# A unit of 192 tokens as the decays' frame, two visits of TensorE a unit, and one named order for a whole program of linear attention and gated MLP

## The chip, the cores and the metric

The kernel runs on one core of a Trainium2 chip. A core has a matrix engine (TensorE, "PE" in the profile; its weight loads run beside the products and are listed as "PEld"), a vector engine (VectorE, "DVE"), a scalar engine (ScalarE, "ACT"), GpSimd ("POOL") and SyncE ("SP"), which here issues the DMA transfers. Each engine works through its own instructions in order; semaphores make one wait for another. Products land in PSUM, which the kernel divides into named banks; all else lives in SBUF.

The metric is the device time of one execution in microseconds. Three runs of the kernel before gave 649.77, 648.35 and 648.44; the median is 648.44.

## The reference

Linear attention with a decay of its own for every feature, and behind it a gated MLP. There are 4 batches, 8 heads, 768 tokens and 48 features a head; the decays alpha lie between 0.8 and 1.0.

```python
for t in range(S):
    state = alpha[:, :, t, :, None] * state + np.einsum('bhd,bhe->bhde', k[:, :, t], v[:, :, t])
    y[:, :, t] = np.einsum('bhd,bhde->bhe', q[:, :, t], state)
x = y.transpose(0, 2, 1, 3).reshape(B * S, H * D)         # 3072 x 384
g = x @ w_gate                                            # 384 x 1536
out = (g * (1.0 / (1.0 + np.exp(-g))) * (x @ w_val)) @ w_out
```

The weights arrive as float64, all else as float32.

## The kernel before, in words

**Attention.** The tokens of a batch are cut into units of 192 tokens (`T`), four a batch and 16 in all; a unit has three chunks of 64 (`C`, `NU`). The eight heads go as four pairs (`G`): in every tile the features of the even head lie on partitions 0 to 47 and those of the odd head on 64 to 111. Inside a frame of tokens the recurrence has a closed form: the key of a token is multiplied by the decays from it to the frame's end, the query of a token is divided by its own decays to the frame's end, and what is left are masked products of 64 by 64 scores; the state before the frame is decayed over the whole frame first. Here the frame is the chunk. For every unit, alpha, k and q are loaded and turned so that tokens run along the columns (L300 on VectorE, L313 on TensorE for the first block); alpha is clamped to 1 ± `ALPHA_DEV` (L347); the first factor of each chunk is taken out (L355, tile `af`), a backward scan gives the keys' factors (L369, tile `Gs`), a reciprocal of each chunk's whole factor feeds the forward scan (L384, in `AT`), keys and queries are multiplied by their factors (L381 on GpSimd or L708 on VectorE; L404), and `Pt` holds the decay over each chunk.

**A chunk** then goes through these steps. The decayed keys are turned to rows, 64 tokens by 48 features (`k_rows` L426 on VectorE: 8 transposes a chunk; the early units on TensorE, L410, with copies on ScalarE). `scores` (L437, L438) makes four pairs of products, even and odd heads side by side, into the bank `sps_bank`; `causal` (L444, VectorE, 2 instructions) masks them into the tile `X` that also holds the decayed queries. `carry` (L470, L471) makes the state after the chunk: the operand `K` holds the keys' rows and an identity, `V` holds the values and the state before, so one product adds both. It goes to the second half of the bank `yps`, and `decay` (L459, VectorE, 2 instructions) multiplies it by `Pt` into the `V` of the next chunk. `outputs` (L479, L480) makes the chunk's outputs from `X` and `V` into the first half of `yps`; ScalarE rounds them (`rows_hi` L487) and VectorE takes what is left over (`rows_lo` L491). When a unit's three chunks are done, ten small DMAs (`repack`, L538; units 0 and 1 go over TensorE instead) put its outputs, heads together, into `xT`, the MLP's input.

**The MLP** works on blocks of 384 tokens, two units each; there are eight. A block has 12 tiles of 128 hidden features, so there are 96 hidden steps. Every float32 operand is split into a high and a low part in float32r, and a product is the sum of three (high by high, high by low, low by high). A hidden step is a gate product `g` and a value product `v` of 9 matmuls of 128 x 384 each (L555), silu on ScalarE (L563), the product with `v` on VectorE (`hidden` L567), the high part on ScalarE (L571), the low part `hl` (L577) on GpSimd in 82 steps and on VectorE in 14, and an out product of 9 matmuls (L596) into three banks. The first two blocks take turns, 7 and 5 tiles at a time, so that weights are wanted at half the pace; what their first 7 tiles gave goes to DRAM and back. The weights come as float64 and are cut to two float32r parts by VectorE (L93, L96, L99), ScalarE (L239) and GpSimd or VectorE (L243), while the first steps run.

**The order.** The work of the first 24 steps, of units 0 to 6 and of all weights stands in a string `ORDER`: each word names an engine (t TensorE, v VectorE, s ScalarE, g GpSimd, y SyncE) and a piece of work, and each engine gets its words in that order. A number and a star are products of 128 x 256 that nobody reads (L667), 131 in all, where TensorE would have little to do. From step 24 on the rest is written as closures, six slots a unit (`stages`, `preps`), spread over nine of a block's twelve steps, and a scheduler of the language's own framework orders the instructions among them. These lines spread it:

```python
for u in range(WU + 1, nun + 1):
    for i in range(2 * NU):
        slots.append(stages(u - 1)[i] + (preps(u)[i] if u < nun else []))
```

All loads and stores go through SyncE's queue.

## Time and profile before

| What | Before |
|---|---|
| median of three runs | 648.44 us |
| profiled execution: span from first to last instruction | 646.5 us |
| TensorE (PE) busy | 607.9 us, 94% |
| VectorE (DVE) busy | 442.3 us, 68% |
| ScalarE (ACT) busy | 238.5 us, 37% |
| GpSimd (POOL) busy | 244.4 us, 38% |
| first gate product of the MLP | 54.1 us into the span |
| gate products' group (L555) | 864 matmuls, 339 ns each by the profile |

The profile is that of one execution, whose span is the time from its first to its last instruction; the median of the runs stands 1.9 us above it. The page gives the busy time of each engine, its share of the span and how many instructions it holds. Matmuls are pipelined, and the end that the profile gives one is modelled: what one of them costs the stream is read from the distance between two starts, not from its length. Groups of instructions read `line engine operation out<-in, shape, count | busy us, mean ns of one | idle time just before them <- what ended most of it`. In the timeline a row is the start in us, the length, engine, line, operation, tiles, shape and, where several follow one another without a break, their count.

### The profile page before, as it was taken

Reading aid. Unit: us, or ns where it says so; the run is one execution under the profiler, and the core shown is the slowest. Engines: PE = TensorE matmul, PEld = TensorE weight load, DVE = VectorE, ACT = ScalarE, POOL = GpSimd, SP = SyncE. Lnnn points to the kernel's source line nnn. Section 1 sums busy time; section 2 is a strip of 40 time slices with the busy share of each in tenths; the row PEclk is TensorE's granted clock in tenths of the full one; section 3 lists DMA queues with packets and bytes.
Section 4 is the critical chain, followed back from the end, with each engine's and each line's share of the span. In section 5 each row is a group of like instructions: output and inputs, shape, how many; then the busy total and the mean of one; then the engine's idle time right before and its main releaser. Section 6 shows DMA issues by size and latency. Waiting matters only on the chain.

```text
span 646.5 us, 13108 instructions
## 1 busy us (share of the span) xinstructions
PE 607.9 (94%) x5097; PEld 553.3 (86%) x5097; DVE 442.3 (68%) x863; ACT 238.5 (37%) x511; POOL 244.4 (38%) x234
## 2 busy tenths in 40 slices
PE   8988797997998999899999999899999999999995
PEld 5768676897897898898989999798989999999995
DVE  6889999999896886965597648865597745311111
ACT  5757576774333132324223331324213221212211
POOL 6225394213111434563355536353355532112120
PEclk9989779999999999999999999899999999999999
DMA  9989953422137432432142512433142211011001
GB/s 210 201 234 258 296 145 74 114 63 69 39 98 194 113 99 49 113 89 65 51 114 59 130 50 63 97 83 71 50 113 64 56 50 39 1 37 38 1 1 42
DMA packets 89286, 60.32 MB, mean 93 GB/s; under 512 B 41600, under 2 KB 87680, under 8 KB 89216
## 3 DMA queue, kind: packets, MB, share of 16 engines
q1 hardware_dynamic: 89216, 59.41, 37.8%
q8 instruction: 42, 0.69, 0.5%
q14 instruction: 28, 0.23, 0.1%
HBM read 45.22 MB, written 5.90 MB: 79 GB/s over the span
## 4 chain that ended last, share of the span: by engine, by line
PE 56%; DVE 14%; SPq 3%; DMA 2%; issue 2%; ACT 1%; POOL 0%; DVEq 0%; ACTq 0%
PE ops L596 18%; PE v L555 16%; PE g L555 16%; DVE K L426 3%; PE sps_bank L437 2%; SPq L538 2%; PE yps L479 2%; PE yps L470 2%; DVE Gs L369 1%; DMA L<-in_alpha_dram 1%; DVE h L567 1%; DVE AT L300 1%; DVE trk L300 1%; DVE V L459 1%; DVE X L444 1%
## 5 line engine op out<-in xcount | busy, mean ns | idle before, releaser
L555 PE MATMUL v<-xT,w 128*128 128x384 f32 x864 | 171.8, 342 | 7.1 <-DVE h L567 7.1
L555 PE MATMUL g<-xT,w 128*128 128x384 f32 x864 | 169.8, 339 | 2.6 <-ACT h L563 2.6
L596 PE MATMUL ops<-w,hh 128*128 128x384 f32 x576 | 167.0, 347 | 0.7 <-POOL w L243 0.7
L555 PEld LDWEIGHTS v<-xT,w 128*128 128x128 f32 x864 | 151.0, 190 | 10.6 <-DVE h L567 7.1
L577 POOL TENSOR_TENSOR hl<-h,hh 128x384 fp32r<-128x384 f32 x82 | 87.1, 1062 | 190.4 <-ACT hh L571 188.4
L555 PEld LDWEIGHTS g<-xT,w 128*128 128x128 f32 x864 | 151.0, 188 | 4.3 <-ACT h L563 3.0
L567 DVE TENSOR_TENSOR h<-h,v 128x384 f32<-128x384 f32 x96 | 52.8, 550 | 135.9 <-PE v L555 132.3
L596 PEld LDWEIGHTS ops<-w,hh 128*128 128x128 f32 x576 | 105.6, 189 | 4.6 <-POOL w L243 1.5
L571 ACT CAST hh<-h 128x384 fp32r<-128x384 f32 x96 | 49.2, 512 | 158.8 <-DVE h L567 153.0
L404 POOL TENSOR_TENSOR X<-trq,AT 48x256 f32<-48x256 f32 x75 | 60.4, 807 | 117.0 <-PE yps L480 78.2
L596 PE MATMUL ops<-w,hl 128*128 128x384 f32 x288 | 98.5, 342 | 2.8 <-DVE hl L577 2.1
L563 ACT ACTIVATE h<-g 128x384 f32<-128x384 f32 x96 | 47.1, 490 | 99.0 <-PE g L555 91.2
L426 DVE STREAM_TRANSPOSE K<-Gs 32x128 f32<-32x128 f32 x240 | 72.7, 303 | 10.7 <-PE yps L471 5.4
L596 PEld LDWEIGHTS ops<-w,hl 128*128 128x128 f32 x288 | 54.5, 189 | 4.9 <-DVE hl L577 3.0
L487 ACT CAST Y<-yps 112x256 fp32r<-112x256 f32 x48 | 17.8, 371 | 76.5 <-DVE V L459 49.4
L444 DVE TENSOR_TENSOR X<-sps_bank,mask 64x256 f32<-64x256 f32 x96 | 40.5, 422 | 4.9 <-PE sps_bank L438 2.3
L437 PEld LDWEIGHTS sps_bank<-X,Gs 48*64 48x64 f32 x384 | 28.3, 139 | 14.2 <-issue 10.0
L437 PE MATMUL sps_bank<-X,Gs 48*64 48x64 f32 x384 | 37.6, 232 | 1.9 <-DVE X L444 1.9
L381 POOL TENSOR_TENSOR Gs<-trk,Gs 128x768 f32<-128x768 f32 x9 | 29.9, 3317 | 19.7 <-DVE Pt L374 19.7
L438 PE MATMUL sps_bank<-X,Gs 48*64 48x64 f32 x384 | 36.3, 231 | 0.2 <-POOL X L404 0.2
L243 POOL TENSOR_TENSOR w<-t,w 128x768 fp32r<-128x768 f32 (+1 forms) x14 | 27.0, 1930 | 21.5 <-ACT w L239 18.0
L479 PE MATMUL yps<-X,V 128*48 128x64 f32 x384 | 31.5, 225 | 3.0 <-DVE X L444 2.2
(109 smaller groups left out, 758.7 us busy)
## 6 DMA issues: line engine op xcount, KB each, us to landing
xT<-Y SPq DMA_DIRECT2D x84, 72.0 KB, 2.2
raw<-in_moe_w_gate_dram SPq DMA_DIRECT2D x12, 384.0 KB, 5.6
raw<-in_moe_w_val_dram SPq DMA_DIRECT2D x12, 384.0 KB, 5.6
raw<-in_moe_w_out_dram SPq DMA_DIRECT2D x12, 384.0 KB, 5.8
V<-in_v_dram SPq DMA_DIRECT2D x96, 48.0 KB, 2.5
L<-in_alpha_dram SPq DMA_DIRECT2D x28, 144.0 KB, 3.3
L<-in_k_dram SPq DMA_DIRECT2D x28, 144.0 KB, 3.0
L<-in_q_dram SPq DMA_DIRECT2D x28, 144.0 KB, 2.8
```

The source lines that it names most:

```text
L404: eng.tensor_tensor(out=X[r, :, j, :], in0=QT[r, :, cs], in1=Fs[r, :, cs], op=ALU.mult)
L426: nc.vector.transpose(out=Ks[(1 - j) * BO + y : (1 - j) * BO + y + 32, :, j, x : x + 32], in_=Kg[j * BO + x : j * BO + x + 32, :, c * C + ...
L437: nc.tensor.matmul(sps[BO : BO + C, g, :], KTt[0:D, cs], X[0:D, g, 0, :], start=True, stop=True)
L438: nc.tensor.matmul(sps[0:C, g, :], KTt[BO : BO + D, cs], X[BO : BO + D, g, 1, :], start=True, stop=True)
L444: nc.vector.tensor_tensor(out=X[r, :, j, :], in0=sps[r], in1=mask[r].unsqueeze(1).to_broadcast([C, G, C]), op=ALU.mult)
L479: nc.tensor.matmul(yps[0:D, g, 0:C], Vd[:, g, 0, :], X[:, g, 0, :], start=True, stop=True)
L555: nc.tensor.matmul(pt, wsp[kind, f][a][:, kt * P : (kt + 1) * P], xT[blk][:, b_, kt, :], start=(n == 0), stop=(n == 3 * KT - 1),)
L563: nc.scalar.activation(h, acc.pop(("g", blk, f)), AF.Silu)
L567: nc.vector.tensor_tensor(out=h, in0=h, in1=acc.pop(("v", blk, f)), op=ALU.mult)
L571: nc.scalar.copy(out=hh, in_=acc["h", blk, f])
L577: eng.tensor_tensor(out=hl, in0=acc.pop(("h", blk, f)), in1=hh.bitcast(F32), op=ALU.subtract)
L596: nc.tensor.matmul(ops[blk][i], h[b_][:, i * P : (i + 1) * P], wsp["o", f][a], start=(first and n == 0), stop=(last and n == 2),)
```

## The change

The frame of the decays becomes the unit of 192 tokens. The scans start and end at unit bounds (`inj` is filled at every 192nd column, no longer at every 64th), so `af` and `Pt` have one column a pair instead of three, and `ALPHA_DEV` goes from 0.25 to 0.21. Inside a unit a chunk's state needs no decay: it is the state before plus the chunk's keys by values.

- `scores(u)` makes the three chunks' products in one piece (12 pairs, L467 and L468), into two banks (`A0`, half of `A1`).
- `carry(u)` follows (L482, L485): the three chunks' keys by values into parts of `A1` and `A2`, without the state; `K` holds only keys' rows and has one buffer, and `V` holds the values of a whole unit with the state in rows that the product leaves out.
- `causal` is four instructions a unit, two over two chunks (L495, 64 x 512) and two over one (L500, 64 x 256).
- `advance(u, c)` (L514, 2 instructions a chunk) adds the state before the chunk to the carry, into the next chunk's rows of `V`, and for the last chunk into a tile `SE`; in a batch's first unit the first one is a copy (L512), done by ScalarE in all four batches. `decay(u)` (L520), once a unit, multiplies `SE` by `Pt` into the next unit's `V`, on VectorE or GpSimd as the order says.
- `outputs(u)` (L535, L536) makes the three chunks' outputs in one piece, into `A0` and `A1` again, so it waits for the masks and additions of its unit; `rows_hi` and `rows_lo` are two instructions each a unit (L553, L557), written over `X` from unit 2 on.
- `k_rows` turns a unit's keys in 8 transposes of 32 x 384 (L444) from unit 5 on; units 0 to 4 are turned on TensorE. The query products are two a unit (L418).
- The values of a unit are loaded in 6 DMAs at once (L364), when the order says so.

`ORDER` names everything, all 16 units and 96 steps; `stages`, `preps`, the slots and the scheduler's part are gone. Each word names the engine of its work, the low parts of the hidden layer among them (`hl`, 49 on VectorE and 47 on GpSimd), and of the stores of output rows. There are 194 products of 128 x 256 that nobody reads instead of 131, and four of 128 x 512 ahead of the first work.

The hidden layer's products, their splitting and the number of steps stay as they are. This is the core of the diff, with "..." where lines are left out:

```diff
-ALPHA_DEV = 0.25
+ALPHA_DEV = 0.21
...
-    NL, NX, NV, NK, NOT, NY, NTS, WSINGLE = 2, 3, 4, 2, 3, 2, 2, 3
+    NL, NX, NV, NK, NOT, NTS, WSINGLE = 2, 2, 2, 1, 2, 2, 3
...
-    Xt = [cp.tile([P, G, 2, C], F32, name=f"X{i}") for i in range(NX)]
+    Xt = [cp.tile([P, 2, G, T], F32, name=f"X{i}") for i in range(NX)]
...
-        nc.vector.memset(inj[:, C - 1 : W : C], 1.0)
+        nc.vector.memset(inj[:, T - 1 : W : T], 1.0)
...
+    def k_rows(u, i):
+        Ks = k_tile(u)
+        Kg = state[u]["Gs"].rearrange("r (g c t) -> r c g t", g=G, c=NU)
+        j, x = i // 2, 32 * (i % 2)
+        for y in range(0, C, 32):
+            nc.vector.transpose(
+                out=Ks[(1 - j) * BO + y : (1 - j) * BO + y + 32, :, :, x : x + 32],
+                in_=Kg[j * BO + x : j * BO + x + 32, :, :, y : y + 32],
+            )
...
-    def scores(u, c):
+    def scores(u):
...
+        s01 = ps.tile([P, G, 2, C], F32, tag="A0", name=f"s01_{u}")
+        st["A1"] = ps.tile([P, 512], F32, tag="A1", name=f"A1_{u}")
...
+        for c in range(NU):
+            sps = st["sps"][c]
             for g in range(G):
...
+    def carry(u):
...
+        A2 = ps.tile([P, 512], F32, tag="A2", name=f"A2_{u}")
...
+        for c in range(NU - last_of_batch(u)):
+            cps = st["cps"][c]
+            for g in range(G):
+                nc.tensor.matmul(
+                    cps[0:D, g, :], Ks[BO : BO + C, c, g, 0:D], Vd[BO : BO + C, c, g, VC[0]], start=True, stop=True
+                )
+                nc.tensor.matmul(
+                    cps[BO : BO + D, g, :], Ks[0:C, c, g, 0:D], Vd[0:C, c, g, VC[1]], start=True, stop=True
+                )
...
-        if not last_of_batch(u, c):
-            for g in range(G):
-                nc.tensor.matmul(sts[0:D, g, :], Ks[:, g, 0, 0:D], Vd[:, g, 0, :], start=True, stop=True)
...
+    def advance(u, c, eng):
...
+            to = Vd[r, c + 1, :, VC[j]] if c + 1 < NU else SE[r]
...
+                eng.tensor_tensor(out=to, in0=cps[r], in1=Vd[r, c, :, VC[j]], op=ALU.add)
...
+    def outputs(u):
...
+        y01 = ps.tile([P, G, 2, C], F32, tag="A0", name=f"y01_{u}")
+        y2 = ps.tile([P, G, 1, C], F32, tag="A1", name=f"y2_{u}")
...
-    def stages(u):
...
-    for s in range(WS, nsteps + 2):
...
```

What this makes of the engines' instructions is shown at three places. First TensorE, before, around hidden step 25: a gate product (9 matmuls of `g`), pieces of one chunk's scores (`sps_bank`), and the value product between them.

```order
L555 MATMUL g_1_4210<-xT_3628,w_637 128x384 x9
L437 MATMUL sps_bank<-X_96,Gs_3771 64x64
L438 MATMUL sps_bank<-X_96,Gs_3771 64x64
L555 MATMUL v_1_4222<-xT_3628,w_788 128x384 x9
L437 MATMUL sps_bank<-X_96,Gs_3771 64x64
L438 MATMUL sps_bank<-X_96,Gs_3771 64x64
```

After the change TensorE reads thus where unit 12's carries end, at hidden step 64 (the names `A_12` are the three banks, `V` and `K` the unit's values and key rows); 24 instructions of scores and 24 of carries stand ahead of these rows without a product of the MLP among them.

```order
L482 MATMUL A_12_5081<-V_99,K_109 48x48
L485 MATMUL A_12_5081<-V_99,K_109 48x48
L608 MATMUL g_4_5108<-xT_4549,w_1204 128x384 x9
L608 MATMUL v_4_5124<-xT_4549,w_1204 128x384 x9
L608 MATMUL g_5_5137<-xT_4549,w_1311 128x384 x9
L608 MATMUL v_5_5154<-xT_4549,w_1341 128x384 x9
```

A chunk's scores stood in pieces among the products of the MLP; a unit's scores and carries now stand in one piece, and the unit's outputs some products later.

VectorE before, near hidden step 30: turned keys in two buffers (`K_114`, `K_113`), the decay of a chunk's state (`V`), the masks of another chunk (`X`), a whole load turned (`trq`), a low part of outputs (`Y`) and the MLP's hidden product (`h`).

```order
L426 STREAM_TRANSPOSE K_114<-Gs_4195 32x4x32 x8
L426 STREAM_TRANSPOSE K_114<-Gs_4562 32x4x32
L459 TENSOR_TENSOR V_103<-yps,Pt_4199 48x4x48 x2
L426 STREAM_TRANSPOSE K_114<-Gs_4562 32x4x32 x4
L444 TENSOR_TENSOR X_96<-sps_bank,mask 64x4x64 x2
L426 STREAM_TRANSPOSE K_114<-Gs_4562 32x4x32 x3
L300 STREAM_TRANSPOSE trq_4652<-L_71 128x4x6x32
L491 TENSOR_TENSOR Y_4555<-yps,Y_4555 112x4x64
L567 TENSOR_TENSOR h_6_4612<-h_6_4612,v_6_4614 128x384
```

VectorE after, at hidden step 52: the masks of unit 10 over two chunks and over one, keys of unit 11 turned at the width of three chunks (`K_109`), two hidden products, and the additions of the state to the carries (`V<-A_10,V`, and `SE`).

```order
L495 TENSOR_TENSOR X_95<-s_10_4320,mask 64x4x128 x2
L444 STREAM_TRANSPOSE K_109<-Gs_4045 32x12x32 x2
L500 TENSOR_TENSOR X_95<-A_10_4321,mask 64x4x64
L620 TENSOR_TENSOR h_4_4295<-h_4_4295,v_4_4380 128x384
L500 TENSOR_TENSOR X_95<-A_10_4321,mask 64x4x64
L444 STREAM_TRANSPOSE K_109<-Gs_4045 32x12x32 x2
L514 TENSOR_TENSOR V_99<-A_10_4321,V_99 48x4x48 x2
L444 STREAM_TRANSPOSE K_109<-Gs_4045 32x12x32 x2
L620 TENSOR_TENSOR h_5_4377<-h_5_4377,v_5_4408 128x384
L514 TENSOR_TENSOR V_99<-A_10_4351,V_99 48x4x48 x2
```

The masks are wider and fewer, the decay in each chunk has become an addition, key rows come in wider transposes, and all that the unit's outputs wait for stands among keys and hidden products in one queue.

More of the change, by code (lines that the diff above doesn't have):

```diff
@@ L431, in scores @@
[L431 to L443 removed]
+        kps, Ks = state[u].pop(("kps", c)), k_tile(u)
@@ L489, in rows_lo, with rows_of @@
-    def rows_lo(u, c):
-        hi, lo = (state[u]["Y"][:, i, :, c * C : (c + 1) * C] for i in range(2))
-        nc.vector.tensor_tensor(out=lo, in0=yps[0:112, :, 0:C], in1=hi.bitcast(F32), op=ALU.subtract)
-    def stage1(u, c):
-        k_rows(u, c)
-        scores(u, c)
-        causal(u, c)
-    def stage2(u, c):
-        carry(u, c, yps[:, :, C:])
-        outputs(u, c)
-        decay(u, c, yps[:, :, C:])
-        rows_hi(u, c)
-        rows_lo(u, c)
+    def rows_of(u, i, x):
+        cs = slice(0, 2 * C) if i == 0 else slice(2 * C, T)
+        return state[u]["Y"][0:112, x, :, cs].bitcast(F32R), state[u]["yps"][i][0:112].rearrange("r g c t -> r g (c t)")
@@ L734, in named_unit @@
+            todo[f"ad{u}.{c}"] = lambda eng, c=c: advance(u, c, eng)
+        for i in range(4):
+            todo[f"kr{u}.{i}"] = lambda eng, i=i: k_rows(u, i)
+            todo[f"ma{u}.{i}"] = lambda eng, i=i: causal(u, i)
+        todo[f"de{u}"] = lambda eng: decay(u, eng)
+        todo[f"S{u}"] = lambda eng: scores(u)
+        todo[f"B{u}"] = lambda eng: carry(u)
+        todo[f"Y{u}"] = lambda eng: outputs(u)
         for kt in range(KT):
-            todo[f"R{u}{kt}"] = lambda eng, kt=kt: pe_repack(u, kt)
@@ L772, in main_path @@
         named_weights(p)
-    for s in range(WS):
+    for s in range(len(steps)):
         named_step(s)
```

490 lines of the change are left out of this document (231 added, 259 removed).

## The prediction

> **What bounds the kernel now.** I read the page's totals first, then the busy time by stage, then single visits of TensorE to the attention in the timeline, then VectorE's groups.
>
> ```profile
> PE 607.9 (94%) x5097; PEld 553.3 (86%) x5097; DVE 442.3 (68%) x863; ACT 238.5 (37%) x511; POOL 244.4 (38%) x234
> ```
>
> TensorE has no slack over the whole span of 646.5 us. The stages differ, so I cut the span where hidden step 0 and step 17 begin their value products and where the last one does. Columns are the stretch, its length, busy time of each engine, granted clock, DMA.
>
> ```profile
> 0.00:55.80 55.80, 48.13 (x515) 35.78 (x516) 45.13 (x90) 33.80 (x81) 19.59 (x47) 0.97 0.97 218
> 55.80:171.50 115.70, 100.15 (x814) 89.95 (x814) 111.53 (x156) 72.55 (x147) 47.66 (x32) 0.94 0.52 131
> 171.50:634.60 463.10, 454.75 (x3746) 423.13 (x3745) 283.94 (x616) 130.22 (x279) 177.18 (x156) 1.00 0.28 70
> 634.60:646.50 11.90, 4.88 (x28) 4.45 (x26) 1.67 (x3) 1.96 (x4) 0.00 (x0) 0.92 0.17 57
> ```
>
> In the second stretch VectorE is busy 111.5 of 115.7 us (96%): it cuts float64 weights while it prepares units, and it sets the pace. In the third TensorE is busy 454.8 of 463.1 us and VectorE 61%: there TensorE sets the pace. So VectorE work counts from 56 to 171 us, TensorE work from 171 us on.
>
> What a hidden step costs on TensorE alone stands near the end, where no attention is left; these are the first gate products of steps 87 and 88:
>
> ```profile
> 595.58 0.33 PE L555 MATMUL g<-xT,w 128*128 128x384 f32 x1
> ...
> 600.26 0.33 PE L555 MATMUL g<-xT,w 128*128 128x384 f32 x1
> ```
>
> 27 products in 4.68 us, 0.1733 us each. The change leaves all 96 steps as they are. The gate products of steps 24 and 84 bound a long stretch that holds some 30 chunks:
>
> ```profile
> 220.09 0.51 PE L555 MATMUL g<-xT,w 128*128 128x384 f32 x2
> ...
> 581.42 0.33 PE L555 MATMUL g<-xT,w 128*128 128x384 f32 x1
> ```
>
> 361.3 us less 60 steps of 4.68 us leaves 80.5 us, or 8.05 us per 192 tokens of attention. A visit for the scores of one chunk, and one for its carry and outputs, read thus:
>
> ```profile
> 556.05 1.72 PE L555 MATMUL v<-xT,w 128*128 128x384 f32 x9
> 557.70 0.27 PE L437 MATMUL sps_bank<-X,Gs 48*64 48x64 f32 x1
> 557.81 0.22 PE L437 MATMUL sps_bank<-X,Gs 48*64 48x64 f32 x1
> ...
> 558.16 0.22 PE L437 MATMUL sps_bank<-X,Gs 48*64 48x64 f32 x1
> 558.31 0.45 PE L596 MATMUL ops<-w,hh 128*128 128x384 f32 x1
> 558.60 0.34 PE L596 MATMUL ops<-w,hl 128*128 128x384 f32 x1
> ```
>
> ```profile
> 552.45 0.34 PE L596 MATMUL ops<-w,hl 128*128 128x384 f32 x1
> 552.80 0.21 PE L470 MATMUL yps<-V,K 128*48 128x48 f32 x1
> ...
> 553.07 0.21 PE L470 MATMUL yps<-V,K 128*48 128x48 f32 x1
> 553.12 0.22 PE L479 MATMUL yps<-X,V 128*48 128x64 f32 x1
> ...
> 553.51 0.22 PE L479 MATMUL yps<-X,V 128*48 128x64 f32 x1
> 553.67 0.61 PE L596 MATMUL ops<-w,hh 128*128 128x384 f32 x2
> ```
>
> Nine products from 556.05 end their turn at 557.61. The next product starts at 558.31 and its follower 0.29 later, not 0.17: the visit cost 0.70 + 0.11 = 0.81 us. Eight pairs (each float32 product is two instructions, even and odd heads side by side) make the stream, six steps from 557.81 to 558.16, 0.058 us a pair, 0.46 in all. So **0.35 us is the price of entering and leaving**, whatever the visit holds. In the second visit carry pairs step by 0.045 us (six steps from 552.80 to 553.07) and output pairs by 0.056 (seven from 553.12 to 553.51); 552.62 to 553.67 is 1.05 us, 1.15 with the slow follower. A unit done in six clean visits is 3 × (0.81 + 1.15) = 5.9 us. The 2.15 us that the measured 8.05 holds beyond that are visits cut in two by products and waits, such as this one of a carry for the outputs of the chunk before in its bank (waiting line, releaser, total, times, longest):
>
> ```profile
> PE yps L470 <- DVE Y L491: 4.0, 5, 1.4
> ```
>
> **The change, part by part.** First TensorE after step 17. A unit now has one visit of scores and carries, 0.35 + 24 × 0.058 + 24 × 0.045 = 2.8 us, and one of outputs, 0.35 + 24 × 0.056 = 1.7: 4.5 us, against 8.05. The instruction counts per unit stay; what goes is four entries, the cuts, and the wait of a carry for the state, since the carry no longer holds the state and VectorE adds it later. If going from scores to carries cost a whole entry more, a unit would be 4.85. By the named order, outputs of unit 4 and units 5 to 15 come after value product 17: 1.7 + 11 × 4.5 less three carries left out at ends of batches (8 × 0.045 each) = 50 us. With value product 17, 78 further gate and value pairs and 80 out products, 237 × 9 × 0.1733 = 369.7 us of hidden layer are left, so 420 us. Before, the same end was reached thus:
>
> ```profile
> 171.46 0.33 PE L555 MATMUL v<-xT,w 128*128 128x384 f32 x1
> ...
> 639.14 0.34 PE L596 MATMUL ops<-w,hh 128*128 128x384 f32 x1
> ```
>
> That is 467.9 us, with four more out products pending (6.2 us) and 92 us of attention for 34 chunks.
>
> Then VectorE. These groups carry its count (count, busy us, mean ns):
>
> ```profile
> L426 DVE STREAM_TRANSPOSE K<-Gs 32x128 f32<-32x128 f32 x240 | 72.7, 303 | 10.7 <-PE yps L471 5.4 <-PE yps L470 1.1
> L567 DVE TENSOR_TENSOR h<-h,v 128x384 f32<-128x384 f32 x96 | 52.8, 550 | 135.9 <-PE v L555 132.3 <-ACT h L563 2.6 <-issue 0.8
> L444 DVE TENSOR_TENSOR X<-sps_bank,mask 64x256 f32<-64x256 f32 x96 | 40.5, 422 | 4.9 <-PE sps_bank L438 2.3 <-PE sps_bank L667 0.7
> L369 DVE TENSOR_TENSOR_SCAN Gs<-AT,inj 128x768 f32<-128x768 f32 x16 | 31.2, 1953 | 0.7 <-PE kps L410 0.2
> L459 DVE TENSOR_TENSOR V<-yps,Pt 48x192 f32<-48x192 f32 x76 | 27.0, 355 | 3.6 <-PE yps L480 2.4 <-PE yps L471 0.2
> L300 DVE STREAM_TRANSPOSE trk<-L 128x768 f32<-128x768 f32 x14 | 22.4, 1604 | 0.0
> L96 DVE SCALAR_TENSOR_TENSOR t<-raw,t 128x768 uint32<-128x768 uint32 x16 | 19.6, 1223 | 0.3
> L93 DVE TENSOR_SCALAR t<-raw 128x768 uint32<-128x768 uint32 x16 | 11.3, 706 | 0.1
> L577 DVE TENSOR_TENSOR hl<-h,hh 128x384 fp32r<-128x384 f32 x14 | 9.2, 658 | 1.3 <-ACT hh L571 1.2
> L708 DVE TENSOR_TENSOR Gs<-trk,Gs 128x768 f32<-128x768 f32 x2 | 1.9, 942 | 0.0
> ```
>
> Widths 192, 256, 384 and 768 at 355, 422, 550 and 942 ns lie on one line: 0.155 us and 1.04 ns an element. So the causal products of a unit, six of 256 before, are two of 512 (0.69) and two of 256: 2.2 us, 0.3 less. The low parts of the outputs save 0.15, the decays become additions of the same width and save nothing. Key rows turn in 8 transposes of 384 instead of 24 of 128. The rows at 128 and 768 put one at 0.82 us, 6.6 for a unit against 7.3; if nothing were saved it is 0.91. I take 0.82. Low parts of the hidden layer move from GpSimd to VectorE, 49 instead of 14 by the order: 35 × 0.55 (the width's price; the row's 0.66 would make it 23) = 19 us more. So VectorE does not get less to do over the whole; what matters is where.
>
> Between hidden products 0 and 17, counted in both orders: 8 causal products for 22 (4 × 0.69 + 4 × 0.42 against 22 × 0.42) −4.9; 12 additions for 16 decays −1.4; 8 whole transposes for 9 −1.6; 3 low parts of weights for 5 (0.95 by width) −1.9; 3 wide query products for 8 narrow ones (0.94, 0.42) −0.6; 4 low parts of outputs for 8 −1.1; one key product (0.94) and one clamp (0.65, an estimate between the 0.71 row and 0.55) less −1.6; one low part of the hidden layer less −0.6; two passes of the weight cut more, +1.9. Together −11.8 us; part of it only moved behind step 17. TensorE needs 92 us there (50 products of 1.56 us, 11 for attention, a few for fillers and turned keys), so VectorE stays the pace: 115.7 − 11.8, about 104 us. Bounds: 97 (TensorE and some waits) and 110 (half the saving lost in waits).
>
> From hidden product 17 to 40 VectorE has in the new order 32 key transposes (26), 14 whole ones (22), 23 hidden products and 17 low parts (22), 8 scans (15), 18 additions and 4 decays (8), 6 query products (6), 12 causal products (7), 8 low parts of outputs (4) and smaller things (8): 118 us. TensorE needs 123: 69 products of 1.56, the outputs of unit 4 and three units. The slack is nearly gone there. GpSimd gives up the low parts and keeps clamps, decays and weights, off the path. For waits from step 17 on I add 12 us: of the 92 us above 25 are beyond 34 clean chunks of 1.96, and I take half of it for waits (ends 4 and 24).
>
> Start to first value product: VectorE's list up to hidden product 0 differs by under 1 us between the orders. It was busy 45.1 of 55.8 us; 10.7 us were chains and loads. Fillers now stand ahead of the first turned loads, and a unit's chain has one round trip to VectorE instead of three. I take 56 us; half of the idle time gained or lost gives 51 and 61. SyncE's weight loads now stand behind loads that wait for a free buffer, which I cost at nothing: this stretch moved 218 GB/s, and the order cuts the last weights past step 13; a late one would fall within these ends.
>
> The end after the last product start, 7.2 us, stays. **Sum:** 56 + 104 + 420 + 12 + 7.2 = 599 us of span. The median of the runs, 648.44, is 1.9 us over the span of the profiled execution, so 601 us.
>
> **Rivals.** (1) VectorE remains the bound to step 40: nothing saved in the second stretch (116) and 8 us more than TensorE needs in the next. 56 + 116 + 428 + 12 + 7 + 2 = 621 us. For: 118 against 123 us; GpSimd's share stays high. Against: its busy share was 61% there.
>
> (2) The visits are not cheaper because the cost lies in the stream, not the entry: 8.05 us stays per unit, 601 + 11 × 3.55 = 640 us. The 0.35 us read off above speaks against it.
>
> (3) In the carries the two heads of a pair now use different rows of the array (keys at 64 to 127 and at 0 to 63) and write one bank; if they took turns, each pair would be 0.045 longer: 38 chunks × 8 × 0.045 = 14 us, 615 us. The scores of before have the same shape, two row halves and one bank, and step by 0.058 us like the outputs, which use all rows. The Trainium skill, TensorEngine Tiling (Array Packing), section Gotcha 1: PSUM Pressure, says that different row tiles cannot access the same bank at once. By that rule this rival holds; the scores in this trace do not follow it.
>
> (4) Slower: TensorE, in order, stands at each unit's outputs until VectorE has masked the scores and added two states: 2.2 + 4 × 0.355 = 3.6 us after the scores. The cover is the carries (1.05) and the products put between: two (3.1 us) at units 9 and 15, three at 3, 5, 7, 11 and 13, at least four elsewhere. The narrowest has 0.5 us to spare, so VectorE's queue running late is seen at once. It decides from (648 − 601) / 14 = 3.4 us a unit; at 4 us, 657 us. For: hidden products and key transposes stand in the same queue. Against: VectorE idles 39% of that stretch now.
>
> **How the numbers follow.** Forecast 0.70 (582 to 618 with the ends above), rival 1 0.15, rival 2 0.04, rival 3 0.03, rival 4 0.06, and 0.02 that it falls under the range. 0.3% is about what a measurement of this kernel tells from no change. Rivals 1 and 3 are still faster, and rival 2 too; between rival 2 and 4 lies a small 0.02. So faster 0.92, same 0.02, slower 0.06. The range 580 to 624 leaves out the ends of rival 1, and rivals 2 and 4.
>
> **What would show it.** In the new profile two visits a unit of 2.8 and 1.7 us between products; step 17's value product near 159 us, the last product start near 591; carry pairs 0.045 us apart; wide key transposes at 0.82 us. Outputs waiting for causal products or additions by more than 1 us a unit would make it wrong upward, a first value product past 62 us also; VectorE idle between 56 and 159 us would say that its count was not the pace.

## The result, and the profile after

The changed kernel takes 624.5 us, the median of four runs (621.91 to 628.15), against 648.58 for the kernel before. The ratio of the runs is given as 0.9646, with a 95% interval from 0.9603 to 0.9689 (it is not the plain quotient of the two medians, 0.9629): 3.5% faster. The prediction was 601 us (580 to 624): the sign was right, the gain half of what was forecast, and the time lies just above the range. The profiled execution of 624.59 us has a span of 621.9.

First the page's totals of the changed kernel, then its busy time by the prediction's stages (first value product, value product 17, last product).

```profile
PE 580.6 (93%) x5152; PEld 552.6 (89%) x5152; DVE 444.6 (71%) x696; ACT 233.3 (38%) x492; POOL 179.2 (29%) x147
```

```profile
0.00:63.70 63.70, 54.34 (x663) 44.57 (x663) 44.75 (x79) 30.79 (x74) 26.38 (x39) 0.89 0.93 217
63.70:180.90 117.20, 100.33 (x775) 93.26 (x773) 113.02 (x141) 75.14 (x155) 51.96 (x33) 0.96 0.45 120
180.90:615.00 434.10, 425.53 (x3719) 414.64 (x3718) 286.34 (x477) 126.92 (x263) 100.89 (x76) 1.00 0.29 73
```

| Stage | Before | Predicted | After | After less predicted |
|---|---|---|---|---|
| start to first value product | 55.8 | 56 | 63.7 | +7.7 |
| to value product 17 | 115.7 | 104 | 117.2 | +13.2 |
| to the last product | 467.6 | 432 | 434.1 | +2.1 |
| to the end | 7.4 | 7.2 | 6.9 | -0.3 |

The third stage gave 33.5 of the 35.6 us that were forecast. The first two gave back 9.4 us, where 11.5 had been expected to be won: of the 22.7 us by which the span was missed, 20.9 lie ahead of value product 17.

How the third stage is made shows in single visits. These rows of TensorE's timeline in the changed kernel hold both visits to one unit (scores and carries, then outputs), with the products around them.

```profile
464.78 0.69 PE L608 MATMUL v<-xT,w 128*128 128x384 f32 x3
465.40 0.27 PE L467 MATMUL s<-X,Gs 48*64 48x64 f32 x1
...
466.80 0.22 PE L468 MATMUL A<-X,Gs 48*64 48x64 f32 x1
466.85 0.20 PE L485 MATMUL A<-V,K 64*48 64x48 f32 x1
466.85 0.20 PE L482 MATMUL A<-V,K 64*48 64x48 f32 x1
...
467.89 0.20 PE L482 MATMUL A<-V,K 64*48 64x48 f32 x1
468.02 0.45 PE L608 MATMUL g<-xT,w 128*128 128x384 f32 x1
...
471.78 1.21 PE L608 MATMUL g<-xT,w 128*128 128x384 f32 x6
472.91 0.27 PE L535 MATMUL y<-X,V 128*64 128x64 f32 x1
...
474.45 0.44 PE L640 MATMUL ops<-w,hh 128*128 128x384 f32 x1
```

Three products from 464.78 end their turn at 465.30; the next product starts at 468.02, 2.72 us later, 2.83 with its slow follower. Six from 471.78 end at 472.82, the next starts at 474.45: 1.63 us, 1.74 with the follower. Forecast were 2.8 and 1.7. From scores to carries (466.80 to 466.85) nothing is paid. All twelve visits for outputs behind step 17 cost this 1.64 us to 0.01, so none waited. What TensorE did wait for from there to the last product (engine, line, releaser; total, times, longest):

```profile
PE v L608 <- DVE h L620: 5.0, 5, 2.6
PE g L608 <- ACT h L616: 3.5, 3, 1.8
```

### The profile page after: what moved, and what is told of

Read it like the earlier page. It is cut to its first block, busy times and chain, and to the rows that moved or that the text cites. A ratio compares the mean times of both kernels' runs of the same rounds, so it can differ in the third digit from the quotient of the medians.

```text
span 621.9 us, 12936 instructions
## 1 busy us (share of the span) xinstructions
PE 580.6 (93%) x5152; PEld 552.6 (89%) x5152; DVE 444.6 (71%) x696; ACT 233.3 (38%) x492; POOL 179.2 (29%) x147
## 4 chain that ended last, share of the span: by engine, by line
PE 56%; DVE 21%; DMA 9%; SPq 6%; issue 4%; ACT 2%; POOL 1%; DVEq 0%; ACTq 0%; POOLq 0%
PE v L608 16%; PE ops L640 15%; PE g L608 14%; DMA L<-in_alpha_dram 4%; DMA L<-in_k_dram 3%; DVE t L142 2%; SPq L592 2%; DVE K L444 2%; DMA V<-in_v_dram 2%; DVE t L145 2%; DVE h L620 2%; PE s L467 2%; PE y L535 1%; DVE t L139 1%; PE early_ps L681 1%
## 5 line engine op out<-in xcount | busy, mean ns | idle before, releaser
L629 POOL TENSOR_TENSOR hl<-h,hh 128x384 fp32r<-128x384 f32 x47 | 52.8, 1122 | 223.2 <-ACT hh L624 207.6
L620 DVE TENSOR_TENSOR h<-h,v 128x384 f32<-128x384 f32 x96 | 52.9, 551 | 88.0 <-PE v L608 82.4
L418 POOL TENSOR_TENSOR X<-trq,AT 48x768 f32<-48x768 f32 x20 | 40.6, 2030 | 79.5 <-DVE trq L335 25.7
L444 DVE STREAM_TRANSPOSE K<-Gs 32x384 f32<-32x384 f32 x88 | 50.1, 570 | 2.1 <-PE A L485 0.5
L629 DVE TENSOR_TENSOR hl<-h,hh 128x384 fp32r<-128x384 f32 x49 | 33.1, 676 | 18.2 <-ACT hh L624 18.0
L374 ACT ACTIVATE dev<-L,nbias 128x576 bf16<-128x576 f32 (+2 forms) x30 | 23.1, 771 | 39.8 <-DMA L<-in_alpha_dram 30.9
L406 DVE TENSOR_TENSOR_SCAN AT<-AT,inj 128x768 f32<-128x768 f32 x16 | 30.9, 1932 | 0.0
L723 POOL TENSOR_TENSOR Gs<-trk,Gs 128x768 f32<-128x768 f32 x8 | 21.8, 2723 | 31.7 <-DVE Pt L401 31.6
L396 DVE TENSOR_TENSOR_SCAN Gs<-AT,inj 128x768 f32<-128x768 f32 x16 | 28.6, 1786 | 0.6
L495 DVE TENSOR_TENSOR X<-s,mask 64x512 f32<-64x512 f32 x32 | 21.9, 685 | 9.6 <-PE s L468 9.2
L335 DVE STREAM_TRANSPOSE trk<-L 128x768 f32<-128x768 f32 x14 | 22.4, 1600 | 8.7 <-DMA L<-in_k_dram 8.6
```

What stands on the lines that cost most here:

```text
L374: nc.scalar.activation(dev, state[u]["La"][r, cs], AF.Abs, bias=nbias[r], scale=1.0)
L396: nc.vector.tensor_tensor_scan(Gs[:, ::-1], AT[:, 1 : W + 1][:, ::-1], inj[:, 0:W][:, ::-1], 0.0, op0=ALU.mult, op1=ALU.add)
L406: nc.vector.tensor_tensor_scan(AT[:, 0:W], AT[:, 0:W], inj[:, T - 1 : T - 1 + W], 0.0, op0=ALU.mult, op1=ALU.add)
L418: eng.tensor_tensor(out=X[r, j, :, :].rearrange("r g t -> r (g t)"), in0=st["QT"][r, :], in1=AT[r, 0:W], op=ALU.mult)
L444: nc.vector.transpose(out=Ks[(1 - j) * BO + y : (1 - j) * BO + y + 32, :, :, x : x + 32], in_=Kg[j * BO + x : j * BO + x + 32, :, :, y : y ...
L620: nc.vector.tensor_tensor(out=h, in0=h, in1=acc.pop(("v", blk, f)), op=ALU.mult)
```

## The experiments

Each kernel is the changed one with the edit shown; times go with the kernel before on the same chip. Three places are asked about: the price of a visit, the start, and the stretch between hidden products 0 and 17.

### The visits cut again

```diff
-t:S12 t:B12 ... t:g64 ... t:v64 ... t:Y12 ... t:g67
+t:S12a ... t:g64 t:S12b ... t:v64 t:B12 ... t:Y12a ... t:g67 t:Y12b
```

In this kernel the carries come behind the turning of the next unit's keys into the single key buffer, so some of them read those rows: part of the sum is another one.

> The changed kernel with the visits of units 5 to 15 cut again: scores of two chunks, an MLP product, scores of the third, a product, the carries; and outputs of two chunks, a product, outputs of the third. Three more visits a unit, the same matmuls. Theory of the prediction, a visit costs 0.35 us whatever it holds: a unit goes from 4.57 to about 5.6 us, 11 units 11.5 us more, time 634 to 637. Rival, the cost lies in the stream alone: 4.57 us a unit, time 623 to 626. If splitting also brings waits of the outputs, more than 637.

643.43 us, ratio 0.9925 (0.9892 to 0.9958): 19 us more than the change. One unit's carries in its timeline (they stand between these two rows):

```profile
487.77 0.68 PE L613 MATMUL v<-xT,w 128*128 128x384 f32 x3
...
489.60 1.84 PE L613 MATMUL g<-xT,w 128*128 128x384 f32 x9
```

The carries' own visit costs 1.31 + 0.11 us (488.29 to 489.60 and the follower), 1.42 in all. The other four read in the same way cost 1.17 (scores of two chunks), 0.71 (of one), 1.17 (outputs of two) and 0.70 (of one), and 0.11 each: a unit of clean visits is 5.6 us, as the theory of the entry price has it, against 4.57. That is 11 of the 19 us. Most of the rest are waits, and not of the carries, which in all eleven units started 0.27 us behind the start of the product ahead of them: value products waited 9.6 us for hidden products instead of 5.0, and gate products 5.9 us for ScalarE instead of 3.5. Cutting costs the entries and, on top, the slack.

### The start

VectorE's longest waits up to the first value product, in the changed kernel:

```profile
DVE V L514 <- ACT V L512: 4.3, 1, 4.3
DVE AT L380 <- PE pt L348: 4.2, 1, 4.2
DVE trk L335 <- DMA L<-in_k_dram: 2.4, 1, 2.4
```

Three suspects: unit 2's loads (ScalarE checks its alpha ahead of the copies of the first state, VectorE turns its keys), TensorE's fillers, and ScalarE's order.

A first try moved unit 2's keys too early in SyncE's order, over unit 1's queries in the same buffer, before these were turned. So in these two kernels unit 2's keys stand in for unit 1's queries, and TensorE's turn of these waits for a later load, which none of the theories meant. They tell nothing of the loads.

```diff
-t:Tk1 y:wl0 v:cl1 y:wl1 ... y:La2 ... t:Tq1 ... y:Lk2
+t:Tk1 y:La2 y:wl0 v:cl1 y:Lk2 y:wl1 ... t:Tq1
```

> The changed kernel with one edit in SyncE's order: the loads of unit 2's alpha and keys go out ahead of the first weights instead of behind three and four of them. In the changed kernel hidden product 0 stands at 69.6 us, the span is 621.9 us. Loads theory: these two loads, which land at about 28 and 35.5 us, hold ScalarE (its check of alpha, ahead of the copies of the first state) and VectorE (4.3 us for those copies, 2.4 us for the keys); without them VectorE loses 6.7 us less, hidden product 0 comes at about 63, the time falls by 5 to 7 us to about 618. Filler theory: TensorE issues 32 and 26 filler products ahead of unit 0's outputs and unit 1's turned keys, so the outputs still start at 29.5; hidden product 0 comes at 68 to 70 and the time stays at 622 to 625.

> Both edits: the loads of unit 2 ahead of the weights, and fewer filler products. If both hold the start, hidden product 0 comes at 58 to 60 us, where the kernel before has it (58.5), and the time is 612 to 614. If only the loads do, as in the loads edit alone (63 and 618); if only the fillers do, as in the filler edit alone. If VectorE's list of work sets the pace to hidden product 17, whatever is won at hidden product 0 is still there at hidden product 17 (182.7 in the changed kernel).

627.8 us (0.9661) and 623.04 us (0.96). The fillers alone:

```diff
-t:4+ t:10* t:Ta0 ... t:11* ... t:18* ... t:32* t:Y0 ... t:26* ... t:33* t:Y1
+t:10* t:Ta0 ... t:3* ... t:6* ... t:10* t:Y0 ... t:10* ... t:12* t:Y1
```

> The changed kernel with fewer filler products ahead of the first gate product: the four of 512 columns gone, 11, 18, 32, 26 and 33 of 256 columns cut to 3, 6, 10, 10 and 12. Filler theory: TensorE, in order, holds the chain; the first turned load starts at about 4.3 us instead of 7.2, hidden product 0 at 62 to 65 instead of 69.6, the time is about 618. Loads theory: VectorE stands at the loads of unit 2 as before, only longer; hidden product 0 within 1.5 us of 69.6 and the time 623 to 626.

622.41 us, 0.9578 (0.9548 to 0.9608). Hidden product 0 came at 66.1 us, but hidden product 17 at 182.5, where the change has it (182.7): VectorE then stood 3.4 us for unit 3's keys. The loads again, now in an order that keeps the buffers:

```diff
-t:Tk1 y:wl0 ... y:La2 ... t:Tq1 ... y:Lk2 ... y:V3 ... y:Lk3
+t:Tk1 y:La2 y:wl0 ... t:Tq1 y:Lk2 ... y:Lk3 y:V3
```

> The changed kernel with three edits in SyncE's order: unit 2's alpha ahead of the first weights, unit 2's keys right behind the turn of the queries whose buffer they take, unit 3's keys ahead of unit 3's values (six transfers). All is computed as in the changed kernel. Loads theory: VectorE's stands for unit 2 (4.3 us for ScalarE's copies behind its check of alpha, 2.4 us for the keys) go, and unit 3's keys are there in time; hidden product 0 at 63 to 65 instead of 69.6, hidden product 17 about 5 us ahead of 182.7, time 617 to 619. Filler theory: outputs of unit 0 still start behind 32 fillers at 29.5; hidden product 0 at 67 to 70, time 622 to 625. Third possibility: the weights, which go out later, are the next wait, then VectorE or TensorE stands at them and hidden product 17 stays within 2 us of 182.7.

> The same three loads moved, and the fillers cut as in the filler run, which alone brought hidden product 0 from 69.6 to 66.1 and lost it again in a wait of 3.4 us for unit 3's keys. If loads and fillers hold the start and VectorE's list sets the pace to hidden product 17: hidden product 0 at 59 to 62, hidden product 17 at 173 to 177, time 613 to 617. If TensorE and the weights hold the stretch behind hidden product 0: it stays at 179 to 182 and the time at 620 to 622.

620.92 us (0.9551) with the loads alone, hidden product 0 at 67.9, 17 at 182.2: the third possibility, the weights are the next wait. 619.98 us (0.9561, 0.9514 to 0.9608) with both, 64.8 and 178.7, between the two cases expected. The 4.3 us wait was still there with the loads moved: ScalarE now stood 6.4 us for the first weight, which its range check wants. So ScalarE's checks were moved, alone and with the others, the first three weights were put ahead of the values, and the change was run again beside them:

```diff
-s:kc0.1 s:w0c ... s:kc0.2 s:cq1 ... s:ck2.0 ... s:ad0.0 ... s:ck2.1 ... s:yh0.1 y:Lq2
+s:kc0.1 ... s:kc0.2 s:cq1 ... s:ad0.0 ... s:yh0.1 s:w0c s:ck2.0 s:ck2.1 y:Lq2
```

> The changed kernel once more, unaltered, beside the three others. Time 622 to 627 as before; hidden product 0 between 65.9 and 70.3 us, where the profiles with this same start had it. If it lies outside, single profiles of the start tell less than taken.

> The changed kernel with one edit in ScalarE's order: its range checks of the first weight and of unit 2's alpha stand behind unit 0's rounded outputs instead of ahead of the last key copies and of the copies of the first state. Theory that ScalarE's queue holds the start (it stood 2.9 us for the first weight, which goes out at 17.2 us instead of 4.9, and 4.5 us more ahead of the check of alpha): VectorE's stand of 4.3 us for those copies falls under 1 us, TensorE's of 2.0 us for the key copies goes; hidden product 0 comes 2 to 5 us earlier than in the unaltered kernel of this call, the time falls by 1 to 4 us. Filler theory: unit 0's outputs start behind 32 fillers anyway; hidden product 0 within 1.5 us.

> All three edits of the start: ScalarE's checks later, the loads of units 2 and 3 earlier, fewer fillers. Without the checks' move hidden product 0 was at 64.8 and the span 616.4. If ScalarE's checks held what was left: hidden product 0 at 59 to 62, hidden product 17 at 174 to 177, time 614 to 618. If VectorE's list from hidden product 0 to 17 (114 us) is what counts, each us won at hidden product 0 is still there at the end. If the start is then held by transfers: hidden product 0 at 64 to 66 and 619 to 621.

> The same with the first three loads of weights ahead of unit 0's values on SyncE's queue, near 6 us instead of 17 to 21 (the kernel before sends its first at 4.9). If late weights hold the first gate product: it comes 2 us or more ahead of the run with the three edits, time 612 to 616. If not (the values and the loads behind them are later in turn): within 1 us of that run or later, time 614 to 620.

The change again: 623.89 us, hidden product 0 at 67.3. Checks moved: 624.85 us and 68.1, no gain; its wait list shows where the 4.3 us went:

```profile
DVE trk L335 <- DMA L<-in_k_dram: 5.7, 1, 5.7
```

With that wait gone, another took its place, here for a transfer. Three edits: 621.22 us (0.96), 66.5, where 59 to 62 was expected of ScalarE's checks. With the weights first as well: 620.28 us (0.961, 0.9561 to 0.9659), 63.2, and the first gate product at 53.6 instead of 59.5. Of the time some 1 us came, not the 6: the two profiles are of the fastest run of the one kernel (617.99 us) and of the slowest of the other (623.6). Why the weights were late in the change can be read in SyncE's queue; first the kernel before, then the change:

```profile
4.86 0.62 SPq L229 DMA_DIRECT2D raw<-in_moe_w_gate_dram  x1
```

```profile
6.58 3.93 SPq L364 DMA_DIRECT2D V<-in_v_dram  x6
...
13.26 3.93 SPq L364 DMA_DIRECT2D V<-in_v_dram  x6
17.23 0.60 SPq L266 DMA_DIRECT2D raw<-in_moe_w_gate_dram  x1
```

Twelve value loads of 48 KB hold the queue 0.65 us each, 7.9 us, and the first weight goes out at 17.2 us instead of 4.9. Meanwhile less is moved: from 10 to 20 us, before and after (the last column is GB/s),

```profile
10.00:20.00 10.00, 10.00 (x71) 7.22 (x71) 6.63 (x13) 4.25 (x13) 4.07 (x6) 1.00 1.17 237
```

```profile
10.00:20.00 10.00, 9.77 (x84) 6.98 (x86) 7.79 (x13) 5.06 (x12) 3.05 (x3) 1.00 0.76 139
```

The last two runs make that one edit alone (shown here), and, in the kernel with all edits of the start, let ScalarE issue unit 0's values instead of SyncE.

```diff
-y:La1 s:ck0.1 ... y:V0 ... y:V1 ... y:wl0 v:cl1 y:wl1 y:wl2
+y:La1 y:wl0 y:wl1 y:wl2 s:ck0.1 ... y:V0 ... y:V1 ... v:cl1
```

> The changed kernel with one edit: the first three loads of weights ahead of unit 0's values on SyncE's queue, at about 6.6 us instead of 17 to 19. If the place of the weights behind twelve value loads holds the start, ScalarE no longer stands for the first weight (2.9 us) and the transfers of unit 2 follow sooner: first gate product at 54 to 57 us (58.5 to 62.6 in the profiles of the unaltered start), time 619 to 622. If the fillers and the check of unit 2's alpha hold it: first gate product at 58 or later and 623 to 626.

> The kernel with all four edits of the start (first gate product at 53.6, hidden product 0 at 63.2, span 615.6), and unit 0's six value loads issued by ScalarE, which has nothing to do until 6 us, instead of SyncE. If SyncE's issue time of 0.65 us each holds what follows, the loads of units 1 and 2 and the weights behind come some 4 us sooner: hidden product 0 at 60 to 62, time 616 to 619. If the transfers themselves are the limit by then: hidden product 0 at 62 to 65 and 619 to 622.

One edit: 622.89 us (0.9611, 0.9573 to 0.9648). The first gate product in the change, and with this edit:

```profile
59.69 1.49 PE L608 MATMUL g<-xT,w 128*128 128x384 f32 x7
```

```profile
54.85 1.86 PE L608 MATMUL g<-xT,w 128*128 128x384 f32 x9
```

Eight profiles with the change's own start put it at 58.5 to 62.6; 54.85 is outside all of them and 0.7 us from the kernel before (54.13). A rival is TensorE's granted clock; up to that product it was 0.91 in this run and 0.89 to 0.94 in the eight, so it does not explain the gain. So the weights' place in SyncE's queue held the first gate product. It is not the only thing that moves this mark: with the loads moved and fewer fillers, and the weights still behind the values, it stood at 55.25. Nor is the mark the time. Hidden product 0 came at 64.9, against 67.0 to 69.6 in four profiles with the change's own order up to it and 58.45 before, and 622.89 us is not clear of the change's 624.5 and 623.9. Values on ScalarE: 620.65 us (0.9574), first gate product at 55.0, hidden product 0 at 65.1: nothing more to be had there. That the transfers are the limit by then fits this, but is not shown.

### Hidden products 0 to 17

VectorE's own marks are its hidden products 0 and 17: at 58.45 and 180.29 in the kernel before, at 69.57 and 182.69 in the change.

```profile
58.45 0.56 DVE L567 TENSOR_TENSOR h<-h,v 128x384 f32<-128x384 f32 x1
...
180.29 0.54 DVE L567 TENSOR_TENSOR h<-h,v 128x384 f32<-128x384 f32 x1
```

```profile
69.57 0.56 DVE L620 TENSOR_TENSOR h<-h,v 128x384 f32<-128x384 f32 x1
...
182.69 0.56 DVE L620 TENSOR_TENSOR h<-h,v 128x384 f32<-128x384 f32 x1
```

The stretch fell from 121.8 to 113.1 us, 8.7 of the forecast 11.8. The second profile of the change has 115.3, and the kernels that alter only the start or later steps 113.3 to 116.4, so 113.1 is the low end of a scatter. What ate the rest stands in the groups of this stretch, the three passes of the weight cut, before and in the change:

```profile
L96 DVE SCALAR_TENSOR_TENSOR t<-raw,t 128x768 uint32<-128x768 uint32 (+1 forms) x15 | 18.2, 1215 | 0.3
L99 DVE SCALAR_TENSOR_TENSOR t<-raw,t 128x768 uint32<-128x768 uint32 x15 | 17.6, 1176 | 0.3
L93 DVE TENSOR_SCALAR t<-raw 128x768 uint32<-128x768 uint32 (+1 forms) x15 | 11.4, 757 | 0.9 <-POOL w L243 0.8
```

```profile
L142 DVE SCALAR_TENSOR_TENSOR t<-raw,t 128x768 uint32<-128x768 uint32 x15 | 23.0, 1534 | 0.5
L145 DVE SCALAR_TENSOR_TENSOR t<-raw,t 128x768 uint32<-128x768 uint32 x16 | 17.0, 1072 | 0.2
L139 DVE TENSOR_SCALAR t<-raw 128x768 uint32<-128x768 uint32 x15 | 13.9, 929 | 0.1
```

That is 47.2 us before and 53.9 after, or 52.9 without the one of L145's sixteen that lies on the edge of the stretch: 5.7 us more, of which 1.9 were forecast. Where GpSimd has nothing to do the first two take 0.96 us and the third 0.55. Beside GpSimd it looks like this (timeline of the change):

```profile
70.53 1.82 POOL L280 TENSOR_TENSOR w<-t,w 128x768 fp32r<-128x768 f32 x1 [3.40 <-ACT w L276]
70.62 2.54 DVE L142 SCALAR_TENSOR_TENSOR t<-raw,t 128x768 uint32<-128x768 uint32 x1
```

VectorE's pass starts 0.09 us behind GpSimd's low part of a weight and ends 0.81 us behind its end. To test it, the low parts were moved:

```diff
-v:w3v2 g:w2p v:h0
+v:w3v2 v:h0 v:w2p
```

and 16 more in the same way.

> The changed kernel with the 17 low parts of weights that GpSimd makes moved to VectorE, 0.95 us each there, 16 us more on its list. Between hidden products 0 and 17 VectorE's three passes of the weight cut take 1.53, 1.08 and 0.93 us on average, though 0.96, 0.96 and 0.55 where nothing runs on GpSimd. Contention theory: VectorE's instructions are drawn out by those of GpSimd beside them, most by these low parts; the passes fall to 1.0 to 1.1, 0.96 and 0.55 to 0.65, 12 us of the 16 come back, the stretch between the two hidden products is 113 to 118 us (113.1 now) and the time 623 to 629. Rival, the passes are slow for another reason (transfers landing beside them, or ScalarE): they keep their means, the stretch is 126 to 130 us, and the time about 638.

```profile
L281 DVE TENSOR_TENSOR w<-t,w 128x768 fp32r<-128x768 f32 (+1 forms) x17 | 18.1, 1064 | 0.0
L143 DVE SCALAR_TENSOR_TENSOR t<-raw,t 128x768 uint32<-128x768 uint32 x15 | 15.8, 1055 | 0.4
L146 DVE SCALAR_TENSOR_TENSOR t<-raw,t 128x768 uint32<-128x768 uint32 x15 | 14.9, 1004 | 0.1
L140 DVE TENSOR_SCALAR t<-raw 128x768 uint32<-128x768 uint32 x15 | 11.9, 791 | 0.2
```

623.67 us (0.9605), the stretch 113.9 us. VectorE has 15 us of low parts more (18.1 against 2.8) and 11 us less of the passes (42.6 against 53.9). The 113.9 us lie within the 113.1 to 116.4 of the kernels with GpSimd's help, so this help was worth next to nothing. The Trainium skill, SBUF — State Buffer, section Who interferes with whom, says that a VectorE instruction with two SBUF inputs contends with a GpSimd instruction that reads SBUF, and that the second one to issue blocks until the first is done. The rows agree: 2.54 us is the rest of GpSimd's 1.82 and most of a pass; and the wide key transposes, with one input, took 566 to 574 ns in all 88 cases, 36 of them with GpSimd busy beside them. But the third pass has one SBUF input as well and was drawn out all the same, from 0.55 to as much as 2.17 us, so two inputs are not the whole condition here.

Does VectorE's list set the pace there? Three kernels take work away: the low parts of weights (replaced by copies on ScalarE), the products by x's low part in steps 0 to 17, and both.

```diff
-            eng.tensor_tensor(out=lo, in0=src, in1=hi.bitcast(F32), op=ALU.subtract)
+            nc.scalar.copy(out=lo, in_=src)
...
+        parts = ((0, 0), (1, 0)) if (blk < 2 and f < HSEG) or (blk == 0 and f < 11) else HL
...
-            for a, b_ in HL:
+            for a, b_ in parts:
```

> The changed kernel with the low parts of the weights left out: ScalarE writes a copy of the weight there in place of the difference that GpSimd (17) and VectorE (3) make, so the MLP's sum is another one; all matmuls stay. It takes 3 us of differences off VectorE's list between hidden products 0 and 17 and, if GpSimd's instructions draw out VectorE's, some 10 us of its weight cut, and adds some 14 us to ScalarE (79 of 117 us busy). If VectorE's list sets the pace there, hidden product 17 comes at 169 to 174 instead of 182.7 and the time is 611 to 616. If TensorE with its waits for transfers and ScalarE sets it, hidden product 17 comes at 179 to 183 and the time is 620 to 625.

> The changed kernel with the products of the weights' high part by the low part of x left out of the gate and value products of steps 0 to 17 (6 matmuls instead of 9, the sum is another one there): 102 matmuls, some 17.7 us, less on TensorE, nothing less on VectorE. In the changed kernel VectorE is busy all the 113.1 us between hidden products 0 and 17. Two-engine theory (VectorE's list needs 113 us there, TensorE's products and its own waits 110 us, as the run without low parts showed): taking from TensorE alone wins 0 to 3 us, hidden product 17 at 179 to 183, time 620 to 625. If TensorE alone sets the pace: 10 us or more, hidden product 17 at 165 to 173, time 607 to 614.

> The same, and the low parts of the weights replaced by copies on ScalarE as in the earlier run, so 18 us off VectorE's time there as well. Two-engine theory: now the stretch from hidden product 0 to 17 falls by 12 us or more below the 113.1 of the changed kernel, to 95 to 101 us, where each alone gave 0 to 3; time 602 to 609. Rival, transfers or a chain of latencies through ScalarE set it: it stays at 107 us or more and the time is 613 to 617 as with the low parts alone.

Busy time between hidden products 0 and 17 (columns as above), less on VectorE, less on TensorE, less on both:

```profile
67.20:177.20 110.00, 99.37 (x764) 93.26 (x762) 91.70 (x130) 84.49 (x168) 23.70 (x18) 0.95 0.46 117
```

```profile
70.30:184.20 113.90, 91.48 (x662) 82.11 (x661) 108.02 (x134) 73.98 (x151) 48.50 (x30) 0.87 0.46 110
```

```profile
65.90:172.40 106.50, 87.92 (x671) 78.86 (x672) 92.01 (x131) 83.96 (x168) 21.97 (x17) 0.92 0.47 121
```

TensorE's 102 matmuls were worth nothing (113.9 us; 624.81 us, 0.9604): VectorE is the pace in the change. The test is weaker than it was meant to be, since at a granted clock of 0.87 TensorE's busy time fell by 5.3 us (from 96.8) and not by 17.7. 17 us off VectorE were worth 3 against the profile of the change (110.0; 616.66 us, 0.9496). Both together were worth 6.6 (106.5; 617.25 us, 0.949, 0.942 to 0.956), so TensorE is right behind VectorE; but 12 had been expected: a third limit lies near 106 us. There VectorE waited 5.7 us for ScalarE, which makes the low parts in that kernel, and 3.3 us for keys, so it is partly the experiment's own; what it would be without stays open.

### Low parts of the hidden layer, and all gains joined

```diff
-v:hl19
+g:hl19
```

and 41 more: all low parts that VectorE had behind step 18.

> The changed kernel with the low parts of the hidden layer from step 18 on given back to GpSimd (42 of them, as before the change most were). They cost VectorE 0.55 to 0.68 us each, some 25 us of its list, 13 of these between hidden products 18 and 40, where VectorE is busy 111 of 128 us. Prediction's view (VectorE has slack from step 17 on, 118 us of work against 123 on TensorE): nothing won, time 623 to 626; GpSimd's low part takes 1.1 us and comes later, so out products may wait and it may be 1 to 3 us slower. Rival, VectorE is the bound to step 40: value product 40 comes 5 us or more ahead of 310.8 and the time is under 619.

623.12 us (0.9582), value product 40 at 310.1 against 310.8. From value product 17 to 40 it took 127.6 us against 129.9 (128.2 to 130.4 in other kernels with that work), so the 25 us taken off VectorE's list behind step 18 were worth some 2 us there at most. The last one joins the moved loads, fewer fillers and the weights' low parts on VectorE:

> A kernel that computes all: the loads of units 2 and 3 earlier, fewer fillers (these two gave hidden product 0 at 64.8 and a span of 616.4), and the low parts of weights that GpSimd makes moved to VectorE (which alone took 1.8 us off the span). If the gains add: hidden product 0 at 62 to 65, hidden product 17 at 175 to 178, time 616 to 619, some 6 to 8 us under the changed kernel (624.5). If VectorE, with 15 us of low parts more and 10 us of contention less, is the tighter engine once the start is shorter: 620 to 623.

623.34 us (0.9567, 0.9516 to 0.9617), hidden product 0 at 67.8 and 17 at 180.2: the gains did not add. The kernels that compute all and have the loads, the fillers or the weights' place altered lie between 620.0 and 623.3 us, each under the change's 624.5 and 623.9. Their intervals overlap the change's (0.9603 to 0.9689) but for one, the moved loads alone (0.9516 to 0.9585), and with further edits of the start these loads overlap it again: that one of the kernels is faster is likely and not shown.

## Why the prediction was right and where it was wrong

- **The price of a visit: right.** Two visits at 2.83 and 1.74 us for 2.8 and 1.7; cut into five, 5.6 us. The entry price was read off two visits of the kernel before, and it carried over.
- **From step 17 on: right.** 434.1 us for 432, of which 369.7 are the hidden layer, 51.6 attention (50 forecast), and 12.8 are left over (12 forecast for waits). The wait list above holds only 8.5 of the 12.8, and the 12 was a guess, half of a remainder: that they agree is luck in part. Giving the low parts back to GpSimd changed 2 us at most there.
- **The start: wrong, +7.7 us**, past the 62 us that the prediction named as a sign. The step that failed is "SyncE's weight loads now stand behind loads that wait for a free buffer, which I cost at nothing". Not the waiting for buffers was the price (SyncE's waits up to 20 us sum to 1.6) but the queue itself: twelve value loads at 0.65 us of issue ahead of the first weight. With the weights ahead of them the first gate product came at 54.9 instead of 59.7 us. Another 2.3 of the 7.7 us lie behind that product: to the first value product the change takes 4.0 us, the kernel before 1.7, because the new order puts unit 2's carries and ten fillers between the two. VectorE's list up to hidden product 0 took 2.7 us more (busy 50.4 for 47.7, forecast under 1), and VectorE idled 19.2 us instead of 10.8. Of the 11.1 us by which hidden product 0 came later, the weights' place gave back 2 to 5; what holds the rest stays open. The granted clock, 0.89 up to the first value product for 0.97 before, is not the whole of it: at 1.00, with all edits of the start, hidden product 0 stood at 63.2 and 65.1.
- **Products 0 to 17: wrong, +13.2 us.** The step is "115.7 − 11.8, about 104 us". It fails twice. Between VectorE's marks 8.7 us were saved, 3.1 less than forecast (5.3 less by the second profile): the passes of the weight cut, drawn out beside GpSimd, took 3.8 us more than the count had them. And the 115.7 us were measured between TensorE's value products though VectorE set the pace. Hidden product 0 stood 2.7 us behind its value product before and 5.9 after, hidden product 17 8.8 us behind before and 1.8 after: a difference of 10.2 us, and 3.1 + 10.2 is the miss. TensorE had run ahead of VectorE at step 17 and no longer did. It now had four more out products in that stretch, 16 for 12 (rows of before and after, out products alone):

```profile
55.80:171.50 115.70, 24.43 (x108) 0.94 0.52 131
```

```profile
63.70:180.90 117.20, 29.33 (x144) 0.96 0.45 120
```

  I took their 6.2 us as won in the next stage; here they stood in TensorE's 92 us, which the sum does not use. That they took the lead is likely and not shown. It is not the amount of work alone: with 102 matmuls less in the stretch, hidden product 17 still stood only 2.8 us behind the start of its value product, and value product 15 had waited 1.3 us for VectorE. The order is the other suspect: it now puts out products 14 and 15 between value products 15 and 17, where the kernel before had 12 to 15 behind value product 17. "TensorE needs 92 us there" was low as well: it was busy 100.3, at a granted clock of 0.96.
- **Wide key transposes: too dear.** 0.57 us each for 0.82. The row at 768 that I interpolated to turns 128 partitions, and these turn 32.

```profile
L444 DVE STREAM_TRANSPOSE K<-Gs 32x384 f32<-32x384 f32 x88 | 50.1, 570 | 2.1 <-PE A L485 0.5
```

- **Rivals.** Rival 1 (621 us) came near the time, with nothing saved in the second stretch, but in part by luck: its start is 7.7 us too short and its last stage 6 too long. Its other half, VectorE as the bound to step 40, is refuted: from value product 17 to 40 the change took 129.9 us against 150.2, and 25 us off VectorE's list won some 2 us at most. Rival 2 fell with the visits. Rival 3 fell too: carries of both row halves start within 0.01 us of each other, write one bank, and step by 0.045 us. By the rule of the Trainium skill, TensorEngine Tiling (Array Packing), Gotcha 1: PSUM Pressure, they would take turns; here they do not. Rival 4 did not occur: no outputs waited.
- **The chances.** Rival 1 with 0.15 was the only case that held a lost saving ahead of step 17. That the start could grow by more than half of its idle time was in no case; with the 61 us end of my own range and 116 for the second stretch the sum is 618, still short of 624.5.

## What to carry to other kernels

Cut a stage at marks of the engine that sets its pace; a saving on one engine between marks of another is blurred by the lead that one has, and work moved across a mark must be charged on the side where it now lies. A transfer that is moved ahead in a queue costs every later transfer its issue time (0.65 us each here), and the first one to feel it is whoever stands first in line for a late load, here ScalarE's range checks, then VectorE. Few long visits of TensorE to a second kind of work are worth their entry price, which one clean visit in the old profile is enough to measure.

## What the runs showed of the hardware that I had not expected

- Beside GpSimd, VectorE's passes with two SBUF inputs took up to 2.65 us instead of 0.96, and the pass with one input up to 2.17 instead of 0.55. Moving 17 of GpSimd's instructions to VectorE therefore left the stretch at 113.9 us, where kernels with GpSimd's help have 113.1 to 116.4.
- With 102 matmuls less, TensorE's granted clock between hidden products 0 and 17 was 0.87 instead of 0.95 (0.92 in the other kernel without them, 0.94 to 0.97 in all that have them), so part of what was taken away came back as slower products.
- With the same order of work, eight profiles put the first gate product anywhere from 58.5 to 62.6 us: at the start, single profiles tell apart only differences above some 4 us.
